# A long convolution cut into two causal halves, with the first half's MLP beside the second half's convolution

## Chip, cores, metric

One NeuronCore of one Trainium2 chip. The metric is device time in microseconds (us) from the first to the last instruction's effect, taken over several executions; the profile is of one of them. PE is the tensor engine (PEld its weight loads), DVE the vector engine, ACT the scalar engine, POOL the GpSimd engine, SP the engine that issues most DMAs. A run is called slow when it is over 1.5% above the fastest of the same kernel. The calls ran on different chips, so kernels of different calls are compared by their ratio to the kernel before. POOL's times in a profile are rough.

## The reference, cut to what matters

The inputs are 2048 positions x 512 channels.

```python
def _A_ref(q, k, v, shift_k, ssm_k, ssm_D):      # on layernorm(x)
    k_shift = sum over t<4 of shifted(k, t) * shift_k[:, ks-1-t]
    kv = k_shift * v
    y  = causal convolution of kv with ssm_k, 2048 taps, by FFT, per channel
    return q * (y + kv * ssm_D)

def _B_ref(x, w1, w2, w3, w4):                    # on layernorm(h)
    h  = gelu(layernorm(x) @ w1)                  # 512 x 512
    hs = h with its four channel groups shifted by 1, -1, 2, -2 positions, @ w2
    x1 = x + hs
    return x1 + gelu(layernorm(x1) @ w3) @ w4     # 512 x 1792 x 512

h   = x + _A_ref(layernorm(x), ...)
out = h + _B_ref(layernorm(h), ...)
```

## The kernel before

The convolution is a transform of length 4096 in two steps, done as matmuls with small cosine and sine tables that the kernel computes at its start. Data of step 1 are re-partitioned by DMA between SBUF and SBUF (the *exchange*), then step 2 follows; filter and signal are each transformed once; the spectra are multiplied; the inverse takes the way back. Every step goes PE, then PSUM, then a copy to SBUF by ACT or DVE. Only after the whole convolution does the MLP start. Its parts (gate, norms, w1, w2, w3, w4) are put in order by a small list scheduler in the kernel (`Plan`), with a cost per task and engine.

The spectrum product and the inverse, for one of 16 frequency groups:

```python
def fwd(kh):
    ps = step2(zk, kh, "psk")                     # 4 matmuls
    a = wk.tile([P, 2, D], BF16, ...)
    evac(a[:], ps[:], 1024, eng="A")              # PSUM to SBUF on ACT
    nc.vector.tensor_tensor(out=pr[:, 0], in0=a[:], in1=gst[:, kh, :, :], op=MUL)      # two
    nc.vector.tensor_tensor(out=pr[:, 1], in0=a[:], in1=gst[:, kh, ::-1, :], op=MUL)   # products
```

The filter is transposed on PE, k by the DMA engines, and the diagonal table of the 4-tap shift is made on POOL:

```python
for c in range(DC):
    nc.sync.dma_start_transpose(kT[:, c, 16:KW], k_r[:, c * P:(c + 1) * P])
# ... cut: index tables on DVE
for c in range(DC):
    for bh in range(2):
        for j in range(8):
            nc.tensor.transpose(pt[:, j, :], hnat[:, c, 8 * bh + j:S:16], ident[:])
        evac(xh[...], pt[:], 1024, fast=True, ...)
nc.gpsimd.tensor_tensor(out=diag..., in0=ident (broadcast), in1=ssk_bf (broadcast), op=MUL)
```

## Time and profile before

The median of the first three runs is 266.6 us (264.63 to 268.69).

| part of the span | what it does | PE busy | DVE busy | ACT busy |
|---|---|---|---|---|
| 0 to 20 us | tables, filter transposes, first step 1 | 13.6 | 17.4 | 8.9 |
| 20 to 109 | convolution | 72.7 of 89 | 62.7 | 64.2 |
| 109 to 155 | gate, norms, w1, w2 | 37.2 of 46 | 39.7 | 31.2 |
| 155 to 264 | w3, w4 | 108.4 of 109 | 42.0 | 39.0 |

The table of windows of the kernel before, from which this is read. Columns: the stretch and its length, busy us (and number) of PE, PEld, DVE, ACT, POOL, then granted TensorE clock (1.00 is full), share of the DMA engines, GB/s.

```profile
...
core 0: us, PE busy (x) PEld busy (x) DVE busy (x) ACT busy (x) POOL busy (x), PEclk, DMA share, GB/s
0.00:20.00 20.00, 13.59 (x134) 7.94 (x138) 17.42 (x41) 8.94 (x11) 6.17 (x20) 1.00 1.00 253
20.00:109.00 89.00, 72.72 (x777) 36.44 (x769) 62.66 (x102) 64.18 (x71) 7.77 (x14) 0.92 0.50 188
109.00:155.00 46.00, 37.22 (x349) 23.33 (x350) 39.66 (x99) 31.18 (x54) 29.64 (x50) 0.89 0.25 90
155.00:264.00 109.00, 108.41 (x549) 51.26 (x547) 42.00 (x83) 39.01 (x66) 10.52 (x18) 1.00 0.06 19
...
```

In the last row PE is busy without a gap: that stretch can only get shorter by less PE work. In the rows above it no engine is full.

The groups of instructions by line of the kernel before: line, engine, operation, out<-in, shapes and count, then busy us and mean ns of one, then idle time before it and what ended it.

```profile
...
L473 DVE TENSOR_TENSOR pr<-asb,rd 128x1024 bf16<-128x1024 bf16 x16 | 11.0, 687 | 3.5 <-ACT asb L339 3.5
L474 DVE TENSOR_TENSOR pr<-asb,rd 128x1024 bf16<-128x1024 bf16 x16 | 11.0, 685 | 0.0
...
L315 DVE TENSOR_TENSOR rt<-a_174,b_176 128x1024 int16<-128x1024 int16 x2 | 5.8, 2922 | 0.0
...
L361 POOL TENSOR_TENSOR diag<-ident,ssk_bf 128x2048 bf16<-128x2048 bf16 x1 | 4.0, 4038 | 3.5 <-DMA ssk_bf<-in_A_shift_k_dram 3.5
...
```

A product of 1024 bf16 elements per partition takes 0.69 us on DVE.

### The profile page before, as it was taken

The page shows a single profiled execution, that of the slowest core. Times are in us where ns is not written, and L with a number is a line of the kernel's source. Part 1 is how long each engine was busy: PE and PEld are TensorE (multiplying, and loading weights), DVE is VectorE, ACT ScalarE, POOL GpSimd, SP SyncE. Part 2 cuts the span into 40 slices and gives each one's busy share as a digit, 9 for nine tenths or more (in the row PEclk, how much of TensorE's full clock was granted, in tenths as well). Part 3 has the DMA queues.
Part 4 walks back from the last instruction along what each step waited for, and adds up shares of the span by engine and source line. Part 5 has one row for each costly group of instructions (what it writes and reads, how often), then busy time and mean ns, then how long its engine had stood idle before and what let it go on. Part 6 is the DMA issues. An engine that isn't in the chain of part 4 may idle for free.

```text
span 266.8 us, 4530 instructions
## 1 busy us (share of the span) xinstructions
PE 231.9 (87%) x1803; PEld 119.0 (45%) x1803; DVE 161.9 (61%) x323; ACT 143.3 (54%) x202; POOL 54.1 (20%) x101
## 2 busy tenths in 40 slices
PE   8665957999579988665988999999999999999994
PEld 3522834555242222224655756445444444444441
DVE  7986807669927998299999994898022250013322
ACT  3638152788479998266867856556500046632000
POOL 3503000000130102029998442251000000000000
PEclk9999995999959999796899999999999999999999
DMA  7999990340701465891000000000011110000111
GB/s 241 249 271 360 407 346 37 142 160 15 295 11 41 153 241 179 295 396 39 1 2 0 4 0 0 2 1 0 2 39 39 39 39 2 0 20 20 42 39 39
DMA packets 18791, 28.08 MB, mean 105 GB/s; under 512 B 10065, under 2 KB 13906, under 8 KB 17234
## 3 DMA queue, kind: packets, MB, share of 16 engines
q1 hardware_dynamic: 17952, 26.74, 29.0%
q0 software_dynamic: 288, 1.05, 1.3%
q8 instruction: 14, 0.23, 0.4%
q10 hardware_dynamic: 530, 0.01, 0.1%
q14 instruction: 7, 0.06, 0.1%
HBM read 11.02 MB, written 2.10 MB: 49 GB/s over the span
## 4 chain that ended last, share of the span: by engine, by line
PE 57%; DVE 24%; DMA 6%; ACT 5%; POOL 4%; issue 2%; ACTq 0%; POOLq 0%
PE mm L717 18%; PE mm L702 18%; DVE st L566 4%; PE pk L406 4%; PE mm L662 3%; DVE rd L571 3%; DMA q_sb<-in_A_q_dram 3%; DMA rd<-rc 2%; DVE rt L315 2%; PE psg L396 2%; DVE vst L342 2%; ACT rc L339 2%; PE psk L396 2%; PE psva L484 2%; DVE pr L474 1%
## 5 line engine op out<-in xcount | busy, mean ns | idle before, releaser
L708 ACT ACTIVATE ra<-mm 128x512 bf16<-128x512 f32 x56 | 33.4, 597 | 49.7 <-PE mm L702 49.6
L702 PE MATMUL mm<-rc,rb 128*128 128x512 bf16 x224 | 50.8, 379 | 0.0
L717 PE MATMUL mm<-rt,ra 128*128 128x512 bf16 x224 | 49.0, 379 | 0.0
L725 DVE TENSOR_TENSOR ob<-mm,rd 128x512 bf16<-128x512 f32 x16 | 11.1, 692 | 61.4 <-PE mm L717 61.4
L717 PEld LDWEIGHTS <-ra 128*128 128x128 bf16 x224 | 22.0, 98 | 26.4
L702 PEld LDWEIGHTS <-rb 128*128 128x128 bf16 x224 | 21.6, 98 | 24.8
L406 PE MATMUL pk<-diag,rb 128*128 128x128 bf16 x256 | 19.8, 238 | 4.4 <-DVE xk L409 4.3
L406 PEld LDWEIGHTS <-rb 128*128 128x128 bf16 x256 | 18.3, 150 | 8.8 <-issue 7.5
L637 PE MATMUL mm<-rc,rf 128*128 128x256 bf16 x128 | 17.8, 295 | 0.0
L530 ACT COPY rc<-ptx 128x512 bf16<-128x512 bf16 x26 | 14.6, 583 | 4.6 <-PE ptx L623 4.6
L662 PE MATMUL mm<-rf,rb 128*128 128x512 bf16 x64 | 16.2, 380 | 1.0 <-ACT rb L643 0.9
L339 ACT CAST asb<-psk 128x1024 bf16<-128x1024 f32 x16 | 16.1, 1030 | 0.5 <-ACT asb L339 0.4
L571 DVE SCALAR_TENSOR_TENSOR rd<-q_sb,qmv,z 128x512 bf16<-128x512 bf16 x16 | 12.7, 792 | 4.6 <-ACT z L560 4.6
L414 DVE BATCH_NORM_STATS2 qst<-q_sb 128x6 f32<-128x512 bf16 x16 | 10.9, 680 | 6.5 <-DMA q_sb<-in_A_q_dram 6.5
L409 DVE TENSOR_TENSOR xk<-pk,rb 128x512 bf16<-128x512 f32 x16 | 10.9, 681 | 6.3 <-PE pk L406 6.2
L560 ACT ACTIVATE z<-mm,qrs 128x512 f32<-128x512 f32 x16 | 10.6, 697 | 7.4 <-PE mm L549 5.7
L637 PEld LDWEIGHTS <-rf 128*128 128x128 bf16 x128 | 13.2, 106 | 2.3
L667 DVE SCALAR_TENSOR_TENSOR q_sb<-rd,cr,mm 128x512 bf16<-128x512 bf16 x16 | 11.7, 733 | 3.7 <-PE mm L662 3.7
L396 PE MATMUL psg<-rd,rf 128*64 128x512 bf16 x64 | 10.3, 418 | 4.2 <-ACT rd L339 4.0
L396 PEld LDWEIGHTS <-rf 128*64 128x64 bf16 x128 | 5.7, 115 | 17.2 <-issue 16.2
L473 DVE TENSOR_TENSOR pr<-asb,rd 128x1024 bf16<-128x1024 bf16 x16 | 11.0, 687 | 3.5 <-ACT asb L339 3.5
L339 ACT CAST rd<-psg 128x1024 bf16<-128x1024 f32 x13 | 13.0, 1028 | 0.0
(224 smaller groups left out, 347.2 us busy)
## 6 DMA issues: line engine op xcount, KB each, us to landing
rd<-rc SPq DMA_DIRECT2D x16, 256.0 KB, 6.0
rc<-ra SPq DMA_DIRECT2D x16, 256.0 KB, 2.4
ra<-vst SPq DMA_DIRECT2D x16, 256.0 KB, 2.4
ra<-in_A_ssm_k_dram SPq DMA_DIRECT2D x4, 512.0 KB, 5.1
rb<-in_A_v_dram SPq DMA_DIRECT2D x2, 1024.0 KB, 8.0
q_sb<-in_A_q_dram SPq DMA_DIRECT2D x2, 1024.0 KB, 8.3
out_dram<-ob SPq DMA_DIRECT2D x16, 128.0 KB, 1.8
rb<-in_B_w_dram SPq DMA_DIRECT2D x1, 1792.0 KB, 7.3
```

The costliest lines, as they stand in the source:

```text
L339: nc.scalar.copy(o, i)
L396: nc.tensor.matmul(ps[64 * t:64 * t + 64, r, :], lhsT=ftab[:, kh, r, t, :], rhs=z[:, kh, t, :], start=True, stop=True)
L406: nc.tensor.matmul(pk[:, c * P:(c + 1) * P], lhsT=kT[:, c, 16 + b - j:KW - 16 + b - j + 1:16], rhs=diag[:, c, j, :], start=(j == 0), stop= ...
L530: nc.scalar.copy(o, i)
L571: nc.vector.scalar_tensor_tensor(out=h_sb[:, b, :], in0=q_sb[:, b, :], scalar=qmv[:, b, 0:1], in1=tl["z", b][:], op0=SUB, op1=MUL)
L637: nc.tensor.matmul(pw_[:, j * 256:(j + 1) * 256], lhsT=w1_sb[:, k, m * P:(m + 1) * P], rhs=hnT[:, k, p * 256:(p + 1) * 256], start=(k == 0 ...
L662: nc.tensor.matmul(px[:], lhsT=shifted(m, b), rhs=w2_sb[:, m, :], start=(m == 0), stop=(m == DC - 1))
L667: nc.vector.scalar_tensor_tensor(out=x1[:, b, :], in0=hbm[:, b, :], scalar=tl["cr", b // 2][:, b % 2:b % 2 + 1], in1=tl["x", b][:], op0=MU ...
L702: nc.tensor.matmul(pg[:], lhsT=w3_sb[:, k, fc * P:(fc + 1) * P], rhs=lnT[:, k, g * 512:(g + 1) * 512], start=(k == 0), stop=(k == DC - 1))
L708: nc.scalar.activation(gbuf[:, g % 2, fc, :], tl["g", g, fc][:], ACT.Gelu_apprx_tanh)
L717: nc.tensor.matmul(po[:], lhsT=gbuf[:, g % 2, fc, i * P:(i + 1) * P], rhs=w4_sb[:, fc, :], start=(fc == 0), stop=(fc == FC - 1))
L725: nc.vector.tensor_tensor(out=ob[:], in0=tl["o", 4 * g + i][:], in1=xh1[:, b, :], op=ADD)
```

## The change

The intent: cut the 2048 positions into two halves of 1024. The first half's output needs only the first half of signal (A0) and filter (F0); the second half's needs A0 with F1 and A1 with F0. Each is a 1024-point transform of complex-twisted data, so tables get smaller and step 2 and the inverse run in tiles of 64x32 and 32x64, eight at a time. The first half's gate, norms and MLP can then run while the second half is still being convolved. The filter arrives transposed and k channel-major from the host, so 64 PE transposes and the DMA transposes go. Nearly everything, also the convolution, is now ordered by the scheduler, with a choice of engine for each task. There are 48 products instead of 32, and the scheduler may put them on DVE or on POOL.

The diff, cut to its core (the whole of it rewrites most of the kernel):

```diff
-    for c in range(DC):
-        nc.sync.dma_start(hnat[:, c, :], A_ssm_k[c * P:(c + 1) * P, :])
-        nc.sync.dma_start_transpose(kT[:, c, 16:KW], k_r[:, c * P:(c + 1) * P])
+    nc.sync.dma_start(fxs[:, 0, 0:4, :], fx[0, 0].rearrange("p (b d) -> p b d", b=4))
+    nc.sync.dma_start(kT[:, 0], kt_r[0])
 # ... cut: new tables; the diagonal table stays one POOL operation
+    nc.gpsimd.tensor_tensor(out=diag..., in0=ident..., in1=ssk..., op=MUL)
+    nc.gpsimd.iota(n2m...); nc.gpsimd.iota(ph...); nc.gpsimd.iota(k8...)   # DVE waits for these
 # ... cut
+    plan = Plan({"ps": 8, "pr": 4, "vs": 2, "z": 2, "hn": 2, "hb": 2, "lb": 2, ...})
+    # step 1 and its copy
+    add(n, {PEc: 0.53}, step1(...), ..., take=[("ps", -1)])
+    add(("E1", sig, b, hp), {A: 0.92, V: 1.14}, ... copy to SBUF ...)
+    # step 2: 16 matmuls into four PSUM banks, and its copies
+    add(n, {PEc: 0.53}, step2(sig, kl), ..., take=[("ps", -2)])
+    add(("E2", sig, kl, t), {A: 0.92, V: 1.14}, ...)        # F1: two V subtract/adds instead
+    # products, on DVE (V) or POOL (GP)
+    def f(e, sl, ...):
+        en = nc.gpsimd if e == GP else nc.vector
+        en.tensor_tensor(out=prs[:, sl[0]], in0=sp[a][:, kl, t], in1=gv, op=MUL)
+    add(("P", s, kl, i, x, t), {V: 0.63, GP: 2.1}, f, ...)
 # ... cut
+    conv(0, [("A0", "F0")])
+    conv(1, [("A0", "F1"), ("A1", "F0")])
+    for s in range(2):                     # half 0's blocks depend on half 0's inverse only
+        for b in range(NB): hblock(s, b)
+        for p in range(4): hpair(s, p); front(s, p)
+    for g, (s, p) in enumerate(((0,0),(0,1),(0,2),(0,3),(1,1),(1,2),(1,0),(1,3))):
+        back(g, s, p)                      # w3, w4
+    # in back(): gelus of every group but the first wait for half 1's products (shared buffer)
 # ... cut: on the host
+    fx = a["A_ssm_k"].T.reshape(2, P, 2, 4 * D).transpose(0, 2, 1, 3)
+    kr = a["A_k"][0].reshape(2 * P, NB, DC, P).transpose(3, 2, 1, 0)
```

## The prediction

> **What bounds the kernel now.** The table of windows splits the 266.8 us into three parts. From 155 to 264 us the tensor engine is busy 108.4 of 109 us: the two big MLP products (448 matmuls; the chain gives 36% of the span to them) run at full rate. From 0 to 109 us (convolution) DVE and ACT are together busy 153 of 218 engine-us, PE with many gaps; the chain of waits shows the reasons: exchange DMA 6.1 us, load of q 7.3 us, index table on DVE 5.7 us, the last inverse exchange 3.5 us. From 109 to 155 us (gate, norms, w1, w2) DVE is busy 39.7 of 46 us and PE only half useful.
>
> **Removed.** 64 filter transposes with 8 evacuations (about 7 us of ACT/DVE), 30 table transposes and their copies (7 us), the int16 index add (5.8 us of DVE), the k transposes by DMA (issued from 2.6 to 15.5 us, ahead of v and q), half of PE's time in step 2 (0.62 us per group of four at two tiles at a time; now eight tiles of 64x32 at a time). The Trainium skill ("TensorEngine Tiling (Array Packing)", Available Configurations) lists 64x32 as 8 tiles; the trace shows four at once (step 1: 8 matmuls of 512 columns in 0.43 us), not yet eight.
>
> **Added.** 16 more products of 1024 (0.60 to 0.69 us each: 10 us DVE), eight subtract/add pairs from PSUM on DVE (about 1.4 us each, against a 1.0 us copy). 80 evacuations of 1024 become 72 (1.01 us ACT, 1.22 DVE). Exchanges keep their bytes (12 MB). A longer chain of small table operations precedes all planned work: DVE waits for POOL's indices, these wait behind the 4 us `diag` and 16 little copies; first evacuation at about 20 us, against 15 before.
>
> **Moved.** Half 0's gate, norms, w1, w2 and only its first w3/w4 group can run beside half 1's convolution: later gelus wait for half 1's products, because their buffer overlays its spectrum. Both are DVE/ACT work: overlap fills gaps but shares two engines.
>
> **Sum.** Engine work in the new kernel, with the trace's durations: PE about 196 us (before about 217), DVE about 170, ACT about 155, including a 20 us start. Before half 1's convolution is done, DVE and ACT need about 42 (start) + 135 (convolution, q statistics) + 60 (half 0's front) + 4 = 240 engine-us; at 88 to 90% use of both that is 135 us. PE then still has about 99 us (seven MLP groups of 12.2 us and half 1's w1, w2), and the tail 3 us. 135 + 99 + 3 is about 237 us. The saving is mostly idle time of DVE/ACT before 155 us (now 30%).
>
> Predicted 237 us, range 222 to 253. Faster by over 2%: 0.91; within 2%: 0.06; slower: 0.03.
>
> **What would show it.** Right: PE near 100% over the last 95 to 105 us; DVE plus ACT at least 85% busy each from 20 to about 130 us; step 2 near 0.5 us per 16 matmuls; first evacuation near 20 us. Wrong: PE gaps over 10 us in the last 100 us (half 1's front late); DVE/ACT below 80% between (exchange latency, SP order, PSUM pairs); 32x64-tile matmuls over 0.8 us per 16.
>
> **What would make it wrong.** The schedule's planned ACT/DVE costs are 8 to 10% below the trace's (0.92 against 1.01, 0.63 against 0.69), an exchange is 2 us (2.4 to 6 here); slips in a fixed order could cost 10 to 20 us. Perfect overlap would give 222.

## The result, and the profile after

| kernel | median | runs |
|---|---|---|
| before | 266.66 us | 264.63 to 268.69 |
| after | 277.45 us | 276.97 to 278.70 |

The ratio is 1.0418, 95% interval 1.034 to 1.0495: slower. (Ratios here are the mean time of one kernel's fast runs over that of the other's fast runs of the same rounds, so not quite the ratio of the medians quoted.)

The table of windows of the kernel after, cut where its stages end; half 1's inverse transform runs from 166.5 to 173.4 us (starts of its first and last matmul):

```profile
...
core 0: us, PE busy (x) PEld busy (x) DVE busy (x) ACT busy (x) POOL busy (x), PEclk, DMA share, GB/s
0.00:20.00 20.00, 9.88 (x36) 4.64 (x37) 14.29 (x60) 4.17 (x7) 9.60 (x34) 0.79 0.92 356
20.00:166.00 146.00, 108.93 (x1292) 53.59 (x1291) 129.73 (x197) 78.24 (x100) 62.16 (x38) 0.81 0.37 129
166.00:173.00 7.00, 6.54 (x60) 4.45 (x62) 4.60 (x9) 4.71 (x9) 0.00 (x0) 1.00 0.01 2
173.00:273.00 100.00, 99.45 (x688) 63.64 (x684) 49.16 (x116) 37.59 (x63) 14.85 (x15) 1.00 0.06 21
...
```

The last row is what was predicted: about 100 us in which PE is full, and some 3 us of tail. The second row is not. The first part should have ended at about 135 us and ended at 173. There DVE is busy 129.7 of 146 us (89%), ACT only 78.2 (54%): together (129.73 + 78.24) of 2 x 146, which is 71%, where the prediction had put 88 to 90% on both. PE has 109 of 146 us and a granted clock of 0.81.

The groups of the kernel after that answer to the products shown for before:

```profile
...
L518 POOL TENSOR_TENSOR r_p<-r_a,r_f 128x1024 bf16<-128x1024 bf16 x14 | 33.4, 2399 | 24.1 <-DMA w4s<-in_w_dram 11.3 <-PE ps L528 8.8 <-ACT r_a L406 3.9
...
L518 DVE TENSOR_TENSOR r_p<-r_a,r_f 128x1024 bf16<-128x1024 bf16 x18 | 26.2, 1481 | 0.9 <-PE ps L528 0.7
...
L518 DVE TENSOR_TENSOR r_p<-r_x,r_f 128x1024 bf16<-128x1024 bf16 x11 | 12.0, 1106 | 2.9 <-PE ps L528 2.9
L518 POOL TENSOR_TENSOR r_p<-r_x,r_f 128x1024 bf16<-128x1024 bf16 x5 | 12.0, 2401 | 0.8 <-PE ps L528 0.7
...
L463 DVE TENSOR_TENSOR r_f<-ps,r_f 128x512 bf16<-128x512 f32 x8 | 5.4, 677 | 0.0
...
L348 DVE TENSOR_SCALAR r_y<-r_y,sv 128x512 int32<-128x512 int32 x2 | 4.4, 2216 | 0.0
...
L326 POOL TENSOR_TENSOR r_dg<-ident,ssk 128x2048 bf16<-128x2048 bf16 x1 | 3.6, 3601 | 3.3 <-DMA ssk<-in_sk_dram 3.3
...
```

The same product on DVE took 0.69 us in the kernel before and takes 1.48 and 1.11 us on average here. A mean can hide two kinds, so look at them one by one. The timeline of POOL and then that of DVE, kernel after, from 79 to 90 us (start, us, engine, line, operation):

```profile
...
78.97 9.25 POOL L518 TENSOR_TENSOR r_p<-r_a,r_f 128x1024 bf16<-128x1024 bf16 x4 [0.90 <-PE ps L528]
```

and DVE:

```profile
...
79.22 4.94 DVE L518 TENSOR_TENSOR r_p<-r_a,r_f 128x1024 bf16<-128x1024 bf16 x2
84.09 0.68 DVE L463 TENSOR_TENSOR r_f<-ps,r_f 128x512 bf16<-128x512 f32 x1
84.69 0.67 DVE L464 TENSOR_TENSOR r_f<-ps,r_f 128x512 bf16<-128x512 f32 x1
...
86.48 2.89 DVE L518 TENSOR_TENSOR r_p<-r_a,r_f 128x1024 bf16<-128x1024 bf16 x2
89.30 0.68 DVE L463 TENSOR_TENSOR r_f<-ps,r_f 128x512 bf16<-128x512 f32 x1
...
```

POOL works on four products from 78.97 to 88.22 us. In that time DVE's first two products take 4.94 us, 2.47 each, instead of 0.68 each; the two products from 86.48 us take 2.89 us together, because POOL is done after the first. Between them the subtract and add of L463 and L464, which read PSUM and SBUF, take their usual 0.68 us beside the same POOL products. The longest DVE product of this run takes 2.60 us. So DVE and POOL do not run these two-input products from SBUF side by side: each waits for the other. The Trainium skill says just this: "SBUF — State Buffer", section "SBUF: two separate sides", describes a port pair that DVE and GpSimd share as an exclusive lock, taken for a whole instruction by a DVE operation with two SBUF inputs (against a GpSimd operation that reads SBUF) or in a 2-port mode; whoever comes second is fully held up. The trace agrees, with 2.47 against 0.68 us. The prediction had counted the 16 additional products as DVE work at 0.60 to 0.69 us each and said nothing of the scheduler's choice to put 19 of the 48 on POOL.

There is a second place. L348 is index arithmetic of 512 elements on DVE, and its mean of 2.2 us hides two kinds as well: one of its two operations starts beside the diagonal table on POOL (L326, 6.0 to 9.6 us) and takes 3.88 us, the other comes after the table and takes 0.55 us.

And a third wait at the start is no lock at all. DVE's timeline again:

```profile
...
18.20 0.92 DVE L384 TENSOR_SCALAR r_y<-n1i,kh,sv 128x32 int32<-128x32 int32 x4 [3.30 <-POOL n1i L376]
...
19.80 1.88 DVE L490 TENSOR_TENSOR r_kv<-ps,r_v 128x512 bf16<-128x512 f32 x3
...
```

DVE sits idle for 3.30 us until POOL has made the index pattern n1i, which stands in POOL's order behind 16 small copies (15.6 to 18.0 us).

What did work: step 2 with eight tiles of 64x32. A line of PE's timeline, kernel after:

```profile
...
59.58 0.63 PE L451 MATMUL ps<-r_a,ftab 64*32 64x512 bf16 x16 [0.43 <-DVE r_k L406]
...
```

16 matmuls of 512 columns end 0.63 us after the first began. The granted clock was 1.00 then; other groups took up to 1.13 us. The kernel before needed 0.62 us for 4 matmuls (two at a time, so two rounds), which make half as much: two PSUM banks instead of four. Eight tiles at a time, which the prediction took from the skill's "TensorEngine Tiling (Array Packing)" and no trace had shown, are now shown. The first planned copy or product comes at 19.8 us, also as predicted.

### The profile page after: what moved, and what is told of

Same layout as the page of the kernel before. It is cut to its first block, busy times and chain, and to the rows that moved or that the text cites. A ratio compares the mean times of both kernels' runs of the same rounds, so it can differ in the third digit from the quotient of the medians.

```text
span 276.0 us, 5175 instructions
## 1 busy us (share of the span) xinstructions
PE 224.8 (81%) x2072; PEld 126.3 (46%) x2072; DVE 198.0 (72%) x380; ACT 124.7 (45%) x177; POOL 86.6 (31%) x87
## 4 chain that ended last, share of the span: by engine, by line
PE 56%; DVE 26%; issue 6%; ACT 4%; DMA 3%; SPq 2%; POOL 1%; ACTq 0%; DVEq 0%
PE ps L759 18%; PE ps L745 15%; DVE r_p L518 6%; PE ps L666 6%; PE ps L695 4%; PE ps L426 4%; PE ps L528 3%; PE ps L641 2%; SPq L440 2%; DVE r_v L604 2%; PE ps L481 2%; DVE hst L608 2%; DVE r_y L348 2%; DVE r_f L464 2%; DVE r_f L463 1%
## 5 line engine op out<-in xcount | busy, mean ns | idle before, releaser
L745 PE MATMUL ps<-r_dg,r_k 128*128 128x256 bf16 x448 | 53.9, 278 | 2.4 <-DVE r_dg L406 2.4
L745 PEld LDWEIGHTS <-r_k 128*128 128x128 bf16 x448 | 43.7, 100 | 13.1 <-issue 6.8
L518 POOL TENSOR_TENSOR r_p<-r_a,r_f 128x1024 bf16<-128x1024 bf16 x14 | 33.4, 2399 | 24.1 <-DMA w4s<-in_w_dram 11.3
L750 ACT ACTIVATE r_x<-ps 128x512 bf16<-128x512 f32 x35 | 20.7, 599 | 28.5 <-PE ps L745 28.5
L759 PE MATMUL ps<-w4s,r_x 128*128 128x512 bf16 x140 | 31.5, 379 | 0.0
L528 PE MATMUL ps<-r_p,ttab 32*64 32x512 bf16 x384 | 21.8, 475 | 8.2 <-DVE r_p L518 3.7
L481 PE MATMUL ps<-r_dg,r_k 128*128 128x256 bf16 (+3 forms) x112 | 19.4, 339 | 9.8 <-POOL r_dg L326 4.9
L518 DVE TENSOR_TENSOR r_p<-r_a,r_f 128x1024 bf16<-128x1024 bf16 x18 | 26.2, 1481 | 0.9 <-PE ps L528 0.7
L406 ACT CAST r_vs<-ps 128x1024 bf16<-128x1024 f32 x14 | 13.6, 1015 | 18.8 <-PE ps L528 13.8
L481 PEld LDWEIGHTS <-r_k 128*128 128x128 bf16 x112 | 11.3, 113 | 19.7 <-issue 11.2
L759 PE MATMUL ps<-w4s,r_kv 128*128 128x512 bf16 x84 | 19.0, 379 | 0.0
L666 PE MATMUL ps<-hnT,r_v 128*128 128x256 bf16 x128 | 16.7, 283 | 0.0
L695 PE MATMUL ps<-r_v,r_h 128*128 128x512 bf16 x64 | 15.6, 380 | 0.0
```

What stands on the lines that cost most here:

```text
L406: (nc.scalar.copy if e == A else nc.vector.tensor_copy)(o, i)
L481: nc.tensor.matmul(o[:, (d + j0) * P:(d + j1 + 1) * P], lhsT=kT[:, s, c, bb, x:x + P], rhs=diag[:, c, j0:j1 + 1, :].rearrange("p j x -> p ...
L518: en.tensor_tensor(out=prs[:, sl[0], :, :], in0=sp[a][:, kl, t, :, :], in1=gv, op=MUL)
L528: nc.tensor.matmul(ps[64 * t:64 * t + 64, bk[h], :], lhsT=ttab[32 * h:32 * h + 32, 2 * kl + t, 2 if x else xx, :], rhs=prs[32 * h:32 * h + ...
L666: nc.tensor.matmul(ps[:, sl[0], j * 256:(j + 1) * 256], lhsT=w1s[:, k, m * P:(m + 1) * P], rhs=hnT[:, k_, k, :], start=(k == 0), stop=(k = ...
L695: nc.tensor.matmul(ps[:, sl[0], :], lhsT=h1T[:, m, bb, x:x + P], rhs=w2s[:, m, :], start=(m == 0), stop=(m == DC - 1))
```

## The experiments

Theory one (lock): products on POOL hold up DVE's and are held up by them; with the slips that follow, this is why the first part is late. Rivals: DVE has simply too much work and POOL relieves it; the exchanges are slower than planned; or the low granted clock lengthens the small matmuls. The lock alone need not explain all: the plan itself ends late too. No run changes the exchanges; in the kernel after they take 2.5 to 4.0 us in the median against the plan's 2.0. Twelve kernels were run. All gave correct results.

| kernel | median us | before, same call | ratio, 95% interval |
|---|---|---|---|
| after | 277.45 | 266.66 | 1.0418 (1.034 to 1.0495) |
| p_on_dve | 263.65 | 268.17 | 0.9864 (0.9775 to 0.9953) |
| p_on_dve_replan | 260.48 | 268.17 | 0.9761 (0.967 to 0.9851) |
| before_pool | 276.38 | 268.17 | 1.0355 (1.0254 to 1.0456) |
| before_host | 264.61 | 268.17 | 0.988 (0.973 to 1.003) |
| before_host_split | 265.46 | 267.04 | 0.9954 (0.988 to 1.0028) |
| evac_on_act | 272.81 | 267.04 | 1.0226 (1.0154 to 1.0297) |
| no_overlap | 275.59 | 267.04 | 1.0345 (1.0275 to 1.0416) |
| start | 256.34 | 267.04 | 0.9617 (0.9544 to 0.969) |
| step2_twice | 259.01 | 267.23 | 0.9709 (0.9638 to 0.978) |
| diag_on_act | 253.56 | 267.23 | 0.9481 (0.9415 to 0.9547) |
| best_guess | 263.94 | 267.23 | 0.9898 (0.9842 to 0.9953) |
| step2_evac_act | 256.08 | 267.71 | 0.9608 (0.9528 to 0.9689) |

### p_on_dve: the same order, all products on DVE

```diff
-                            en = nc.gpsimd if e == GP else nc.vector
+                            en = nc.vector
```

> The kernel after, same planned order, but all 48 spectrum products are issued on DVE (19 of them were on POOL). Lock theory: a POOL product and a DVE product with two SBUF inputs exclude each other (in the profile after, overlapped DVE products took 2.5 us, the others 0.68). Then every DVE product is back at 0.60 to 0.69 us, DVE busy falls from 198 to about 188 us although it does 19 more products, the last product of half 1 ends at about 145 us instead of 158, and the span falls by 8 to 20 us, to 256 to 268. Rival theory: DVE is simply overloaded and POOL relieved it: 19 more products at 0.63 us put 12 us on DVE, and the span rises to about 285 to 289.

The planner still believes in POOL, so order and all other engines stay; only the engine that carries out 19 products changes. Groups of this kernel:

```profile
...
L518 DVE TENSOR_TENSOR r_p<-r_a,r_f 128x1024 bf16<-128x1024 bf16 x32 | 20.7, 681 | 0.4 <-PE ps L528 0.3
...
L518 DVE TENSOR_TENSOR r_p<-r_x,r_f 128x1024 bf16<-128x1024 bf16 x16 | 10.5, 688 | 0.7 <-PE ps L528 0.7
...
```

All 48 products are at 0.68 to 0.69 us. They take 31.2 us; in the kernel after, 29 of them took 38.2. DVE does 19 products more and is busy 185.1 instead of 198.0 us. Half 1's inverse begins at 150.2 instead of 166.5 us, and the median falls by 13.8 us (5.5 points of ratio). The rival, that POOL relieves DVE, expected a rise. It falls. The run takes away two things at once, the lock and POOL's own slower product; but the plan had costed that product at 2.1 us, near its 2.12 us at best, so what the plan did not foresee is the waiting.

### p_on_dve_replan: the planner told so

```diff
-                        add(("P", s, kl, i, x, t), {V: 0.63, GP: 2.1}, f, ...)
+                        add(("P", s, kl, i, x, t), {V: 0.63}, f, ...)
```

> As p_on_dve, but the planner knows that products run on DVE alone and orders anew. Its own sum says 236 us after its zero, against 230 with POOL, and the kernel's zero lies about 18 us after the span's start. Lock theory: no slip is left, so 254 to 260 us, and the convolution part ends close to the plan (last inverse transform at about 18+133 us). Rival theory (slip comes from exchange latency, granted clock or small-tile matmuls): the plan slips by 25 us again, 275 to 285.

260.5 us, just above the expected 254 to 260. Against p_on_dve of the same call this is 3.2 us less, with intervals that overlap. Two rows of its table of windows (columns as above):

```profile
...
20.00:150.00 130.00, 107.20 (x1296) 54.63 (x1297) 116.85 (x220) 74.08 (x95) 19.38 (x20) 0.83 0.41 145
...
157.00:257.00 100.00, 99.00 (x682) 63.37 (x680) 48.48 (x114) 37.15 (x62) 13.13 (x13) 1.00 0.06 21
...
```

Half 1's inverse starts at 149.7 us. From the plan's zero at about 18 us the plan had the end of that inverse at 133, which makes 151; it ended at 156.7. Most of the slip of the kernel after (plan 127 + 18 = 145, measured 173) is gone with the lock. But 157 us is not 135. In the first row DVE is 90% busy and ACT 57%, together (116.85 + 74.08) of 2 x 130, which is 73%.

### before_pool: the lock put into the kernel before

```diff
-        nc.vector.tensor_tensor(out=pr[:, 1, :, :], in0=a[:], in1=gst[:, kh, ::-1, :], op=MUL)
+        (nc.gpsimd if kh % 2 else nc.vector).tensor_tensor(out=pr[:, 1, :, :], in0=a[:], ...)
```

> The kernel before with the second product of every odd step (8 of 32 products) on POOL. Lock theory: POOL products take 2.0 to 2.5 us, DVE products that meet one take about 2.5 instead of 0.69, and the kernel gets 4 to 15 us slower although DVE has 8 fewer products. Rival theory (POOL relieves DVE): 5 us less of DVE work on the chain from 80 to 106 us, so 0 to 5 us faster.

The groups of the products in this kernel:

```profile
...
L473 DVE TENSOR_TENSOR pr<-asb,rd 128x1024 bf16<-128x1024 bf16 x16 | 19.3, 1236 | 1.6 <-ACT asb L339 1.6
...
L474 POOL TENSOR_TENSOR pr<-asb,rd 128x1024 bf16<-128x1024 bf16 x8 | 18.6, 2328 | 15.8 <-ACT asb L339 15.8
...
L474 DVE TENSOR_TENSOR pr<-asb,rd 128x1024 bf16<-128x1024 bf16 x8 | 9.3, 1160 | 0.0
...
```

Eight products left DVE, and DVE's other 24 went from 0.69 to 1.2 us on average: 28.6 us of DVE time where all 32 had taken 22.0. The ratio is 1.0355. The verdict at 2% is unclear, as three of the seven runs of the kernel before were slow; but each run of before_pool (274.69 us or more) is above each of theirs (269.48 or less). The longest DVE product is 2.61 us. The lock shows in the other kernel too, at the size that was expected.

### before_host: only the host layout

```diff
-        nc.sync.dma_start(hnat[:, c, :], A_ssm_k[c * P:(c + 1) * P, :])          # 4 loads, then 64 PE transposes
+        nc.sync.dma_start(xh[:, 4 * g:4 * g + 4, :], A_ssm_k[...])               # from the transposed layout
-        nc.sync.dma_start_transpose(kT[:, c, 16:KW], k_r[:, c * P:(c + 1) * P])
+        nc.sync.dma_start(kT[:, c, 16:KW], A_k[:, c, :])
```

> The kernel before with only the host layout part of the change: the filter comes transposed (64 PE transposes and 8 evacuations gone), k comes channel-major (no DMA transposes). If this part is worth what the prediction costed it at: first step-1 matmul at about 7 instead of 14.5 us, k, v and q landed about 10 us earlier, and 6 to 14 us less in all (253 to 261). If the start is bound by the table chain on DVE instead: 0 to 4 us.

A miss for the prediction's costing: 1.2%, and the interval includes none. The other branch, a start bound by DVE's chain of tables, fits. The first step-1 matmul came at 12.3 instead of 14.5 us, not at 7. Two groups say why in part:

```profile
...
L354 POOL TENSOR_TENSOR diag<-ident,ssk_bf 128x2048 bf16<-128x2048 bf16 x1 | 4.5, 4530 | 4.1 <-DMA ssk_bf<-in_A_shift_k_dram 4.1
...
L317 DVE TENSOR_SCALAR rt<-rt 128x2048 int16<-128x2048 int16 x1 | 4.0, 3975 | 0.0
...
```

L317 masks 2048 int16 elements on DVE. In the kernel before it took 0.69 us (there it came after the POOL operation); here it starts inside the diagonal table's 4.5 us and takes 3.98 us. It has one input, so by the skill's "SBUF — State Buffer" it can only be the other case, a 2-port mode, which the page says such an operation can enter. It held DVE's chain at the start up by 3.3 us.

### before_host_split: the table in four pieces

```diff
-    nc.gpsimd.tensor_tensor(out=diag (all 2048 columns), ...)
+    for c in range(DC):
+        nc.gpsimd.tensor_tensor(out=diag[:, c] (512 columns), ...)
```

> before_host with the diagonal table built in four pieces on POOL. Lock theory: in before_host DVE's masking of 2048 int16 took 3.98 us (0.69 in the kernel before) because the 4.5 us table operation on POOL held it off; in four pieces it takes at most about 1.7 us, the first step-1 matmul comes at 9 to 10 instead of 12.3 us, and the kernel gains 1 to 3 us on before_host. If something else limits the start: 0.

The mask took 1.41 us as expected, and DVE's chain at the start ended about 1.7 us earlier; the first step-1 matmul came at 10.6, not at 9 to 10, because the next DVE operation met the table too (1.25 instead of 0.41 us). The kernel did not get faster (0.9954, not distinguishable from before_host). What is gained before 15 us is lost later in this kernel. Where, was not followed up. The host layout alone is thus worth some 1% in the kernel before; both intervals include none, and before_host's reaches 2.7%.

### start: index patterns first, and the same remedy in the new kernel

```diff
+    nc.gpsimd.iota(n2m...); nc.gpsimd.iota(ph...); nc.gpsimd.iota(k8...); nc.gpsimd.iota(n1i...)   # moved up
-    nc.gpsimd.tensor_tensor(out=diag (all 2048 columns), ...)
+    for c in range(DC):
+        nc.gpsimd.tensor_tensor(out=diag[:, c] (512 columns), ...)
```

> As p_on_dve_replan (same planned order), but on POOL the index patterns come before the diagonal table, and the table is built in four pieces of 512 columns. Lock theory: the two DVE index operations that took 2.2 us each beside the one 3.6 us table operation go back to about 0.6 us; DVE's first planned operation moves from 19.8 to about 14 us, ACT's table load ends at about 16 instead of 21 us, and the span falls by 3 to 6 us (254 to 257). If loads or the first matmuls limit the start instead: no gain.

(On p_on_dve_replan.) 256.3 us, 1.4 points of ratio better; the intervals overlap a little. The first planned DVE operation comes at 16.5 instead of 19.8 us. But the run changed two things, and the timelines say which one did it: DVE's index operations beside the table (L348 and L349, here L355 and L356) end only 0.4 us earlier, because each of them now meets a piece (1.26, 1.34 and 1.41 us), while the wait of 3.3 us for n1i is gone. So the gain here is that of the order on POOL, not of the lock. The lock theory had expected 14 us.

### diag_on_act: the table off POOL

```diff
-        nc.gpsimd.tensor_tensor(out=diag[:, c], in0=ident..., in1=ssk..., op=MUL)
+    nc.scalar.copy(ssf[:], ssk[:])
+    for i in range(4 * DC):
+        nc.scalar.activation(diag[:, i // 4, i % 4, :], ident[:], ACT.Identity, scale=ssf[:, i:i + 1])
```

> As start, but the diagonal table is made by 16 small operations on ACT, which idles there, and no longer on POOL. Lock theory: nothing on POOL holds DVE's index operations any more (in start the two took 1.26 us each and the mask 1.41 us beside four table pieces): DVE's first planned operation comes at 13.5 to 14.5 instead of 16.5 us, and the span falls by 1 to 3 us more (ratio to before 0.950 to 0.958). If the first matmuls wait for the table or for k: no gain.

253.6 us, 5.2% faster than the kernel before and the best of all. The two index operations that took 4.36 us in the kernel after are now, in DVE's timeline (in the kernel before L315, in another form, took 1.22 and 4.63 us, the second beside the table; in before_host, where it came first, the two took 2.35 us together):

```profile
...
6.21 1.00 DVE L356 TENSOR_SCALAR r_y<-r_y,sv 128x512 int32<-128x512 int32 x2
7.25 0.69 DVE L357 TENSOR_SCALAR r_y<-r_y 128x1024 int32<-128x1024 int32 x1
...
13.54 1.88 DVE L492 TENSOR_TENSOR r_kv<-ps,r_v 128x512 bf16<-128x512 f32 x3
...
```

Two operations in 1.00 us instead of 4.4. The first planned operation comes at 13.54 us, 3.0 us earlier than in start: this is what the lock on the table, in its four pieces, costs. The 16 ACT operations take 4.8 us. They are not free: the next ACT operation, a sine whose input is ready at 7.9 us, starts at 10.6; in start it came at 10.9, so nothing is worse than there. The interval just touches that of start.

### no_overlap: half 0's MLP after half 1's convolution

```diff
-                [("hn", s, p)], take=[("hb", 1)])
+                [("hn", s, p)] + ([("I1", 1, b_) for b_ in range(4)] if s == 0 else []), take=[("hb", 1)])
```

> As p_on_dve_replan, but half 0's front (scaled copy, transposes, w1 and all after it) waits for half 1's last inverse transform; the gates and statistics still run early. If running half 0's MLP beside half 1's convolution is worth what the change meant it for, the kernel gets 10 to 18 us slower (plan: 249.8 against 236.1), 270 to 278. If the overlap only shares DVE and ACT, 0 to 5 us slower.

(On p_on_dve_replan.) 275.6 us, 15 us slower, as the plan said. Two rows of its windows:

```profile
...
20.00:130.00 110.00, 79.83 (x1012) 29.01 (x1011) 94.46 (x174) 59.24 (x66) 11.01 (x12) 0.78 0.49 169
...
135.00:271.00 136.00, 134.01 (x998) 91.36 (x993) 68.89 (x165) 61.54 (x104) 19.69 (x21) 1.00 0.05 16
...
```

Without the overlap half 1's inverse ends at 135 us instead of 157, but then PE has 134 us of work left instead of 99. From 20 to 135 us DVE is busy 96.2 and ACT 61.4 us, together 69% of the two; with the overlap it is 74% (below), so the overlap does fill some gaps. The overlap, the idea at the heart of the change, is worth 15 us here; this kernel, which has neither the overlap nor products on POOL, is 3.5% slower than the kernel before. The prediction gave the same 135 us to the first part with half 0's front included; on the chip 135 us is enough only for the convolution without it.

### evac_on_act, step2_evac_act: is DVE's sum the limit?

```diff
-            {A: 0.92, V: 1.14}     # copies after step 1, after step 2, after the inverse
+            {A: 0.92}              # evac_on_act: all three; step2_evac_act: after step 2 only
```

> As p_on_dve_replan, but the copies of 1024 elements out of PSUM (steps 1 and 2, inverse) may run on ACT alone, planned anew. It takes about 25 us of DVE work (planned sum 179 to 154 us) and puts 20 us on ACT, which was idle 40% of the first 140 us. If the first part is limited by the sum of DVE's work, as my pooled sum of both engines supposed, it ends 12 to 20 us earlier: 242 to 250. If it is limited by the chain (step 1, exchange, step 2, product, inverse, exchange, with 4 PSUM banks to each step 2 and inverse), moving load gives nothing: 257 to 263; the planner's own sum says nothing (236.1 both).

> As diag_on_act, but only the copies after the second transform step go to ACT alone (those after step 1 and of the inverse stay free to use either), planned anew; the planner's own sum is 231.6 instead of 236.1. If the first part is limited by DVE's sum where ACT is idle, a partial move helps where the full move of evac_on_act did not: 247 to 251 us, half 1's inverse transform starts at about 137 instead of 141.6 us. If the chain of stages sets the time whichever engine copies: within 2 us of diag_on_act (252 to 256), or worse by a slip of the plan as in best_guess.

evac_on_act (on p_on_dve_replan) is 12.3 us slower, which neither theory expected. Its windows before half 1's inverse:

```profile
...
20.00:160.00 140.00, 113.37 (x1274) 52.75 (x1275) 94.38 (x197) 94.85 (x118) 16.41 (x18) 0.78 0.38 135
...
```

Now DVE and ACT are equally busy, 94.4 and 94.9 of 140 us, together 68%: less than the 73% of p_on_dve_replan, not more. In its timeline the eight copies of one signal after step 1 run on ACT one after another for 7.5 us (55.8 to 63.2 us), DVE waits 6.5 us, and PE's step 2 waits with it. With only one engine to copy, each stage of the chain gets longer. step2_evac_act (on diag_on_act) moves only part: 256.1 against 253.6 us, ratios 0.9608 and 0.9481 with intervals that just touch, so no gain and possibly a loss, although the planner's own sum was 4.5 us better; half 1's inverse starts at 149.0 us, where 137 had been expected if DVE's sum were the limit. So in evac_on_act neither engine's sum sets the first part. In p_on_dve_replan DVE, 90% busy, is not far from full, but both attempts to take copies off it lost at least as much in the chain as they gave. A reading that fits, but that no run isolates: copies come early and could use both engines, products come late and only DVE takes them.

### step2_twice: does the small matmuls' time, and so the clock, count?

```diff
-            for r in range(2):
+            for r in (0, 1, 0, 1):
```

> As start, with all matmuls of every second transform step issued twice (the second pass overwrites the first with the same values, so the result stays right). It measures what small-tile matmul time costs, and with it the low granted clock of the first part (0.61 to 0.71 between 60 and 100 us in start), under which 16 such matmuls take about 1.0 instead of 0.57 us. The 16 groups add 9 us of PE time at full clock, up to 16 at half. If matmul time (and so the clock) is on the chain of the convolution: 8 to 14 us slower than start, a ratio to before of 0.99 to 1.015. If PE waits for copies and products anyway: 0 to 3 us slower, a ratio of 0.96 to 0.973.

(On start.) 259.0 against 256.3 us, 0.9 points of ratio; the intervals of the two overlap. That is within the second branch. But the run did not add what it was meant to add. The window from 20 to 145 us, with the matmuls of the second transform step alone (L452), in start and then in step2_twice (columns: PE and PEld busy, clock, DMA share, GB/s):

```profile
...
20.00:145.00 125.00, 16.71 (x256) 4.16 (x256) 0.86 0.42 148
...
20.00:145.00 125.00, 22.05 (x512) 8.69 (x512) 0.89 0.42 149
...
```

Twice the matmuls took 5.3 us more, not 9 to 16, and half of that (2.7 us) shows at the end. The granted clock rose with them: from 0.61 to 0.77 between 80 and 100 us, from 0.71 to 0.80 between 60 and 80. So the run changed the very clock that it was to test. The granted clock in the first part of start is indeed low (0.61 from 80 to 100 us; it is 1.00 after 140 us), and the skill's "TensorE: Matmul & The Clock Gate", section "What's actually happening", says that half rate is the default and sustained activity lifts it; that the clock rose with more matmuls agrees. The inverse's matmuls were not doubled. What the low clock costs the first part therefore stays open.

### best_guess: a better plan on paper

diag_on_act with copies of transposed activations on ACT alone, another seed and more rounds for the planner, whose own sum was 234.4 instead of 236.1 us.

> diag_on_act with the transposed activations copied out of PSUM by ACT alone, another seed and twice the rounds for the planner: its own sum is 234.4 instead of 236.1. Expected 0 to 3 us better than diag_on_act, 250 to 255 us; no theory hangs on it.

263.9 us: 10 us worse. Half 1's inverse starts at 151.6 us against 141.6. Its first 100 us match those of diag_on_act; between 100 and 160 us PE loses 8 us. A difference of 2 us in the planner's sum predicts nothing. Why this plan slipped was not followed up.

## Why the prediction was wrong

The prediction was 237 us (222 to 253), the result 277.5: 40 us off, and of the wrong sign against the kernel before.

- *PE's last part*, "PE then still has about 99 us ... and the tail 3 us": right. From the last matmul of half 1's inverse to the end of the span it is 276.0 - 173.4 = 102.6 us.
- *The start*, first evacuation near 20 us: right in time (19.8 us). Its cause was half right: it was put down to waits for POOL's indices, and 3.3 us were such a wait, for n1i behind the 16 copies; but another 3.4 us was DVE held by the diagonal table. Taking away the first (start) and then the second (diag_on_act) gave 7 us, which the prediction did not have.
- *Eight tiles at a time*: right, 0.63 us for 16 matmuls. *No filter transposes*: right, but in the kernel before their absence is worth only about 1% (before_host); costing removed operations by their durations did not give what they were worth. One of these durations, the "5.8 us" of the int16 index add, was itself mostly lock: it took 2.35 us where it started before the table did (before_host).
- *"16 more products of 1024 (0.60 to 0.69 us each: 10 us DVE)"*, and so "DVE about 170" us: this step failed. DVE was busy 198.0 us. POOL took 19 of the 48 products, and those of DVE that met them took up to 2.60 us. The diff showed the choice of engine; the prediction passed over it, and did not ask what two engines do to each other. p_on_dve shows the size: 13.8 us, with replanning 17 us (277.45 - 260.48). With all products on DVE it is still busy 185 us, so some 15 of the 28 us above the predicted 170 are not the products' lock; the prediction's split of the work between DVE and ACT was off (below).
- *"The schedule's planned ACT/DVE costs are 8 to 10% below the trace's"*, named as the main risk: not so. Instructions in a row overlap a little: three DVE copies of 1.22 us each take 3.48 us in a row, 1.16 each, against a planned 1.14.
- *"at 88 to 90% use of both that is 135 us"*: this step failed too, and is the rest of the miss, about 23 us (260.5 against 237). The sum of work was right. After the 20 us start, the prediction had 240 - 42 = 198 engine-us left, to be done in 115 us (86% of two engines). In p_on_dve_replan DVE and ACT are busy 122.4 and 79.7 us from 20 to 156.7 us, 202 in sum, but this took 136.7 us: 74%. DVE alone did reach the predicted use, 90%; ACT reached 58%. Over the whole kernel DVE was to have about 170 and ACT 155 us, with 20 of each for the start; measured are 185.4 and 121.2, of which 14.2 and 4.1 fall in the start. The prediction had named its own sign of failure, DVE/ACT below 80%. The kernel before has (62.66 + 64.18 + 39.66 + 31.18) of 2 x 135 from 20 to 155 us, 73%, so the new kernel as a whole uses the two engines no better. A pooled sum assumes that work can go to either engine at any time. The one large move that was tried, about 22 us of work from DVE to ACT (evac_on_act), made the kernel slower. What sets these 73 to 74% (PSUM banks in groups of four, the stage order, the exchanges, the low granted clock, or DVE's own 90%), the runs do not settle.
- *"overlap fills gaps but shares two engines"*: right. The overlap is worth 15 us (no_overlap): PE's last part gets 35 us shorter, the first part 22 us longer. DVE and ACT together go from 69% to 74%.

The change itself holds a gain: with the products on DVE and planned anew, the index patterns first on POOL and the diagonal table on ACT (diag_on_act), it is 5.2% faster than the kernel before, instead of 4.2% slower.

## What to carry to other kernels

Do not give POOL an elementwise product to relieve DVE while DVE has operations with two SBUF inputs: a product took POOL 2.1 to 2.6 us, and DVE's 0.68 us product beside it up to 2.60 us. Look at the same instruction's minimum and maximum in the profile, not only at its mean, whenever two engines that share something run together, and check small setup work on POOL (tables, masks) for the same conflict; ACT made such a table in 4.8 us without holding DVE. A run that changes two things at once (start) needs the timeline to say which of them counted. When estimating a stage of dependent steps from the sum of two engines' work, take the use of those engines from the kernel at hand (here 73% before and 74% in p_on_dve_replan), not a wished 90%, and sum each engine by itself.

## What the Trainium skill lacked or had wrong

- "SBUF — State Buffer", section "SBUF: two separate sides", states the exclusive lock but no numbers for this pair of operations. The runs show: a 1024-element bf16 product takes 0.68 us on DVE and 2.12 us on POOL at best; met by each other, up to 2.60 us (DVE) and up to 2.57 us (POOL). The page has it right that reading PSUM on one side avoids the two-input conflict: 0.68 us beside POOL's products.
- The same page: a DVE operation with a single input is held too, by its 2-port rule. The runs show how much: masking 2048 int16 elements 0.69 us free, 3.98 us beside a POOL table operation; int32 index arithmetic of 512 elements 0.54 us free, 3.88 us beside it.
- "GPSIMD Engine Reference", section "Key points", says that DVE is about 2x faster for elementwise work. For this bf16 product the runs show 2.12 against 0.68 us, a factor of 3.1 before any conflict; here the measurement decides. The page's own measured ratio (1.96) is of an fp32 add, which no run here has. The page names the conflict, but gives no size for what sharing work between the two engines can cost: 19 products moved back gave 13.8 us.
- "TensorEngine Tiling (Array Packing)" gives tile counts; the runs add a time, 0.63 us for 16 matmuls of 64x32 tiles and 512 columns (two rounds of eight) at a granted clock of 1.00.
